# Seven quarter products per two batches: from lagging 64x64 quadrants to the whole TensorE array

## The chip, the cores and the metric

The kernel runs on one core of one Trainium2 chip. The metric is the device time of one execution in microseconds (us), as the median of several; lower is better. Executions of one kernel spread by almost 2%: the timed fast runs of before lie between 395.2 and 402.4 us over all submissions. A verdict needs 2% and a 95% interval from fast runs of the same rounds.

## The reference, cut to what matters

```python
def _attn_ref(q, k, v):                     # 8 batches, 12 heads, 448 tokens, head size 64
    scores = scale * np.matmul(q, k.transpose(0, 1, 3, 2)) - np.log(S)
    attn = 1.0 / (1.0 + np.exp(-scores))    # a sigmoid, no softmax
    return np.matmul(attn, v)

def _moe_ref(x, w_in, w_out):               # 3584 tokens, 768 -> 2048 -> 768
    h = x @ w_in
    g = h * (1.0 / (1.0 + np.exp(-h)))
    return g @ w_out
# x is the attention's output, heads side by side
```

Inputs and output are float32 in memory; the kernel computes in float16 with float32 sums.

## The kernel before

Names that the text uses. A **group** is four heads of one batch; there are 24, three to a batch. **S** is a score step of a group (seven of them; TensorE, then two sigmoids on ScalarE), **V** its values block (28 matmuls, then two evictions on VectorE). Two batches at a time, the first layer is computed with seven **quarter products** (a Strassen-like scheme) for each of eight output blocks: 56 products a pair, for three pairs, and **Q** is one of their matmuls. The second layer is done in 14 units of seven products, and **P** is one of their matmuls. (In the code, `S` is the number of tokens, 448.) The first two batches go through the first layer in the plain way at the start.

The program's order comes from a small scheduler that runs in Python while the kernel is built: it keeps an own clock per engine and issues what its clock says is ready. Its constants are assumptions about the chip, and they fix the order of every in-order queue. A product of 64x64 quadrants runs in two halves, since two row halves of the array may not write one PSUM bank together (the prediction cites where that is said): the upper rows go ahead, and the lower rows follow after a semaphore, mixed with the upper rows of the next product.

```python
    def lower_ready():
        if not fifo:
            return False
        q, c = fifo[0]
        return c > 0 or (q.left is not None and pl.t >= q.left + 700.0)

    def lane_step(p=None, c=0):

        low = fifo.popleft() if lower_ready() else None
        assert p is not None or low is not None
        N = max(([p.N] if p else []) + ([low[0].N] if low else []))

        def go():
            if p:
                p.last = p.mm(0, c)[-1]
            if low:
                if low[1] == 0:
                    wait = nc.tensor.nop()
                    left = low[0].last
                ins = low[0].mm(1, low[1])
                if low[1] == 0:
                    for a_, b_ in ((wait, left), (ins[0], wait)):
                        tc.add_manual_dep(
                            a_.ins, b_.ins.name,
                            mybir.DependencyInfo(mybir.DependencyClass.Sync, mybir.DependencyReason.DATA),
                            reason="the upper rows have left the bank",
                        )

        done = low is not None and low[1] == low[0].n - 1
        d = N / 2.4 + 2.5
        pl.pe(d, low[0].key if done else None, [], go)
        if p:
            fifo.append((p, c))
            pl.main += d * (0.2 if p.n == NQ else 1.0)
            if c == p.n - 1:
                p.left = pl.t

    def emit(p, bank_id, deps):

        p.bank = bank_id
        ff_wait(deps)
        while len(fifo) > (7.5 if p.n == NQ else 2.5 * p.n):
            drain_one()
        for c in range(p.n):
            lane_step(p, c)
            if (c + 1) % 2 == 0 or c == p.n - 1:
                between()


    def between():
        if todo:
            if some_tasks() or todo[0][0][:2] != "tp" or todo[0][1] < NHB * NQ:
                return
        if pl.main >= pace[0] and vis[0] < len(visits):
            if visit():
                pace[0] = max(pace[0] + pace[1], pl.main + 300.0)

```

A quarter product in this form is 3 x 2 x 2 matmuls of 64x64, and attention is visited between them:

```python
            def mm(h, c):
                return [
                    nc.tensor.matmul(
                        bank[64 * j_ : 64 * j_ + 64, :S], lhs[64 * h : 64 * h + 64, c, 64 * j_ : 64 * j_ + 64],
                        rhs[64 * h : 64 * h + 64, c, :],
                        start=(new and c == 0 and h == 0), stop=(h == 1 and c == NQ - 1), skip_group_check=True,
                    )
                    for j_ in range(2)
                ]
# ... the combinations on VectorE, the sigmoids on ScalarE, the products on GpSimd ...
            emit(p, ib, (hold(ib) if new else []) + self.deps_of(j, n))
```

K and Q of the groups 8 to 23 are turned by DMA: VectorE copies them into a staging tile (one for K, one for Q), a DMA transpose on SyncE's queue writes one of two buffers, and the next copy waits for the transpose before it:

```python
            x = (xk, xq)[z][ring(n)]
            dst = (kT, qT)[z][tring(n)]
            y = xp[z]
            lk = ("k", n) if w == "k" else ("q", n, None)
            m = before(n, lambda i: -1 if i in on_pe else 0)
            old = [("tr" + w, m)] if m is not None and m not in on_pe else []
            pl.op(
                "DVE", 530, ("re" + w, n), [lk] + old,
                lambda x=x, y=y: nc.vector.tensor_copy(
                    y.rearrange("p (c j d) -> p c j d", j=2, d=D), x.rearrange("p (j c d) -> p c j d", j=2, d=D)
                ), prio=-1,
            )
            pl.op(
                "SP", 1200, ("tr" + w, n),
                ([("trk", n)] if w == "q" and one else []) + [("re" + w, n)] + freed("S", n, NCH - 1, of=tring),
                lambda dst=dst, y=y: nc.sync.dma_start_transpose(dst, y), nbytes=1300,
            )
# ...
    visits = []
    for n in range(NHB * NQ, NALL):
        if n in on_pe and n >= 8:
            visits[-6:-6] = [("tk", n, 0), ("tq", n, 0)]
        for i in range(NCH):
            if i == 2 and n > NHB * NQ:
                visits.append(("V", n - 1, 0))
            visits.append(("S", n, i))
    visits.append(("V", NALL - 1, 0))
    vis = [0]
```

## Time and profile before

| before | |
|---|---|
| time, 4 runs | 401.38 us median (398.8 to 402.33) |
| profiled execution | 394.43 us, span 392.6, granted clock 0.998 |
| TensorE busy | 94% |
| VectorE, ScalarE, GpSimd busy | 67%, 63%, 36% |

The profiled execution is faster than all four timed ones. That matters later. In the profile, "PE" is TensorE, "PEld" its weight loads, "DVE" VectorE, "ACT" ScalarE, "POOL" GpSimd, "SP" SyncE with most output DMA; "issue" is idle time that no semaphore explains. The view of waits has one line per waiting engine and source line: what it waited for, us in total, times, longest. TensorE's waits of before, from 86 us to the end:

```profile
PE ps L905 <- issue: 5.5, 8, 1.1
PE ps L1028 <- issue: 1.7, 3, 1.1
PE ps L1028 <- DVE us L1042: 1.5, 1, 1.5
```

TensorE stands idle little, and mostly at Q for no reason that the profile names. What the waits can't show is a TensorE that is busy with only half of its rows.

### The profile page before, as it was taken

How to read it: one execution, taken by the hardware profiler on the slowest of the kernel's cores; microseconds unless marked ns; L12 is line 12 of the kernel's file. 1: busy time of each engine (PE TensorE's matmuls, PEld its weight loads, DVE VectorE, ACT ScalarE, POOL GpSimd, SP SyncE). 2: the span in 40 equal slices, each digit the busy share in tenths (PEclk: the TensorE clock that was granted, in tenths of full speed). 3: DMA queues.
4: the chain of work that ended last, by engine and by line, in shares of the span. 5: the costliest groups of instructions: out<-in, count | busy, mean ns of one | idle time of the engine just before them, and what ended most of it. 6: DMA issues, size and time to landing. Idle time of an engine off the chain costs nothing.

```text
span 392.6 us, 17870 instructions
## 1 busy us (share of the span) xinstructions
PE 368.0 (94%) x7724; PEld 292.7 (75%) x7724; DVE 264.2 (67%) x484; ACT 246.3 (63%) x562; POOL 142.2 (36%) x193
## 2 busy tenths in 40 slices
PE   6899999999998999998999998899999989899994
PEld 2677777889786676866887766788787676699993
DVE  2545888989454678877755687768466777775542
ACT  1886788578786967787857576689774456510100
POOL 8745302202222318775222057774000176620000
PEclk9999999999999999999999999999999999999999
DMA  8999995706999981345988907049952200013335
GB/s 103 200 209 203 209 208 87 99 2 103 183 185 207 165 139 27 48 64 72 179 139 153 215 8 92 3 55 156 156 112 56 52 3 3 2 39 88 85 83 122
DMA packets 63741, 42.30 MB, mean 108 GB/s; under 512 B 33712, under 2 KB 62896, under 8 KB 63664
## 3 DMA queue, kind: packets, MB, share of 16 engines
q0 software_dynamic: 25008, 22.81, 39.0%
q1 hardware_dynamic: 38656, 18.36, 24.9%
q8 instruction: 61, 1.00, 1.1%
q14 instruction: 16, 0.13, 0.1%
HBM read 45.61 MB, written 11.01 MB: 144 GB/s over the span
## 4 chain that ended last, share of the span: by engine, by line
PE 78%; DMA 7%; DVE 5%; ACT 5%; issue 4%; POOL 1%; SPq 0%; DVEq 0%; PEldq 0%; ACTq 0%; POOLq 0%
PE ps L1028 30%; PE ps L905 23%; PE ps L802 8%; PE ps L564 8%; PE ps L553 7%; DMA kT<-xp 3%; ACT at L601 2%; DMA xk<-in_k_dram 2%; ACT at L1182 1%; DMA qT<-xp 1%; DMA out_dram<-us 1%; PE ps L512 1%; DVE us L920 1%; ACT gt L706 1%; ACT gt L687 1%
## 5 line engine op out<-in xcount | busy, mean ns | idle before, releaser
L1028 PE MATMUL ps<-wo,gt 64*64 64x384 f16 x1792 | 140.9, 323 | 2.0 <-issue 1.5
L601 ACT ACTIVATE at<-ps 128x448 f16<-128x448 f32 x252 | 118.7, 589 | 29.2 <-PE ps L553 28.7
L1028 PEld LDWEIGHTS <-gt 64*64 64x64 f16 x2240 | 108.3, 107 | 18.4 <-issue 6.5
L711 POOL TENSOR_TENSOR gt<-us,gt 128x448 f16<-128x448 f32 (+4 forms) x96 | 77.2, 827 | 70.4 <-ACT gt L706 55.2
L905 PE MATMUL ps<-xt,wi 64*64 64x448 f16 x864 | 80.3, 350 | 1.6 <-issue 1.1
L1028 PE MATMUL ps<-so,gs 64*64 64x384 f16 x896 | 81.3, 323 | 0.2 <-issue 0.2
L553 PE MATMUL ps<-qT,kT 64*64 64x448 f16 (+2 forms) x728 | 71.5, 333 | 3.8 <-DMA qT<-xp 0.7
L920 DVE SCALAR_TENSOR_TENSOR us<-ps,us 128x448 f32<-128x448 f32 x96 | 58.1, 621 | 22.5 <-PE ps L905 17.0
L905 PEld LDWEIGHTS <-wi 64*64 64x64 f16 x1152 | 55.8, 106 | 20.2 <-issue 9.2
L905 PE MATMUL ps<-xs,ex 64*64 64x448 f16 x576 | 61.3, 351 | 1.6 <-issue 1.4
L1042 DVE TENSOR_TENSOR us<-ps,us 128x384 f32<-128x384 f32 x70 | 38.6, 555 | 34.8 <-PE ps L1028 29.5
L279 POOL DMA_DIRECT2D v<-in_v_dram x22 | 16.0, 727 | 118.1 <-PE ps L564 83.3
L706 ACT ACTIVATE gt<-us 128x448 f16<-128x448 f32 (+4 forms) x96 | 43.0, 484 | 17.5 <-DVE us L920 11.7
L1028 PEld LDWEIGHTS <-gs 64*64 64x64 f16 x896 | 49.7, 107 | 4.9 <-issue 1.1
L553 PEld LDWEIGHTS <-kT 64*64 64x64 f16 x728 | 34.3, 109 | 16.8 <-issue 12.4
L1028 PE MATMUL ps<-so,gt 64*64 64x384 f16 x448 | 43.7, 323 | 1.6 <-DVE us L1042 1.5
L802 PE MATMUL ps<-xt,wi 128*128 128x256 f16 (+1 forms) x384 | 40.9, 260 | 0.2 <-issue 0.2
L1182 ACT ACTIVATE at<-ps 128x384 f16<-128x384 f32 (+3 forms) x78 | 33.1, 532 | 10.3 <-PE ps L553 10.2
L905 PE MATMUL ps<-xs,wi 64*64 64x448 f16 x288 | 36.5, 351 | 2.4 <-issue 2.4
L905 PEld LDWEIGHTS <-ex 64*64 64x64 f16 x576 | 31.5, 106 | 8.3 <-issue 2.7
L564 PE MATMUL ps<-at,v 64*64 64x448 f16 (+2 forms) x688 | 36.8, 331 | 0.2 <-issue 0.2
L802 PEld LDWEIGHTS <-wi 128*128 128x128 f16 x384 | 33.0, 98 | 5.3 <-issue 1.7
(64 smaller groups left out, 424.4 us busy)
## 6 DMA issues: line engine op xcount, KB each, us to landing
out_dram<-us SPq DMA_DIRECT2D x112, 96.0 KB, 3.2
xk<-in_k_dram POOLq DMA_DIRECT2D x22, 224.0 KB, 5.3
v<-in_v_dram POOLq DMA_DIRECT2D x22, 224.0 KB, 4.3
xq<-in_q_dram POOLq DMA_DIRECT2D x20, 224.0 KB, 6.8
wo<-in_moe_w_out_dram POOLq DMA_DIRECT2D x4, 768.0 KB, 14.1
wi<-in_moe_w_in_dram POOLq DMA_DIRECT2D x8, 192.0 KB, 6.9
wi<-in_moe_w_in_dram POOLq DMA_DIRECT2D x4, 384.0 KB, 10.6
ex<-in_k_dram POOLq DMA_DIRECT2D x2, 224.0 KB, 6.7
```

The lines of the kernel that those rows point to most:

```text
L279: lambda: nc.gpsimd.dma_start(v16[vring(n)], src(v, b, g)),
L553: nc.tensor.matmul(pt[r][64 * h : 64 * h + 64, lo : lo + (c1 - c0) * D], kT[tring(n)][64 * r : 64 * r + 64, i, 64 * h : 64 * h + 64], qT[t ...
L564: nc.tensor.matmul(pt[h][64 * j : 64 * j + 64, :N], v16[vring(n)][64 * h : 64 * h + 64, j, c * D : (c + 1) * D], ats[slots[c]][64 * h : 64 ...
L601: lambda r=r: nc.scalar.activation(ats[sl][:, r], pt[r][:, :S], AF.Sigmoid, bias=NEG_LOG_S, scale=QKSCALE),
L706: lambda o=o, x_=x_: nc.scalar.activation(o, x_, AF.Sigmoid, scale=1.0 if in_sb else ISX), prio=0,
L711: lambda o=o, x_=x_: nc.gpsimd.tensor_tensor(o, x_, o, ALU.mult), prio=5,
L802: nc.tensor.matmul(bank[:, z * N : z * N + N], wi[:, cc, fc * P : (fc + 1) * P], x[:, cc, self.c0 : self.c1], start=(cc == 0 and z == 0), ...
L905: nc.tensor.matmul(bank[64 * j_ : 64 * j_ + 64, :S], lhs[64 * h : 64 * h + 64, c, 64 * j_ : 64 * j_ + 64], rhs[64 * h : 64 * h + 64, c, :] ...
L920: lambda: nc.vector.scalar_tensor_tensor(us[o], bank[:, :S], ISX, us[i_], ALU.mult, ALU.add), prio=-2,
L1028: nc.tensor.matmul(bank[64 * j : 64 * j + 64, :HE], lhs[64 * h : 64 * h + 64, c, 64 * j : 64 * j + 64], rhs[64 * h : 64 * h + 64, c, :], s ...
L1042: lambda: nc.vector.tensor_tensor(o, bank[:, :HE], u, add), prio=-2,
L1182: lambda r=r, src_=src_: nc.scalar.activation((at[:, base : base + m] if base < 8 else atx[:, base - 8 : base - 8 + m])[:, :, r, :N], src_ ...
```

## The change

The intent: a quarter product has 128 rows and 128 columns to offer, so it needn't be cut into quadrants. On the whole array there is no lag of rows and a quarter of the instructions. But the tiling mode changes whenever attention, which needs quadrants, comes between, so attention is kept out of those stages. Beside it, constants of the scheduler change.

```diff
-        return c > 0 or (q.left is not None and pl.t >= q.left + 700.0)
+        return c > 0 or (q.left is not None and pl.t >= q.left + 450.0)
 # ... (the same constant in two more places)
-            pl.main += d * (0.2 if p.n == NQ else 1.0)
+            pl.main += d * (0.0 if p.n == NQ else 1.0)
 # ...
-        if pl.main >= pace[0] and vis[0] < len(visits):
+        if pl.main >= pace[0] and vis[0] < len(visits) and (pl.mode == 2 or 0):
             if visit():
 # ...
-            def mm(h, c):
-                return [
+            def go():
+                for c in range(NQ):
                     nc.tensor.matmul(
-                        bank[64 * j_ : 64 * j_ + 64, :S], lhs[64 * h : 64 * h + 64, c, 64 * j_ : 64 * j_ + 64],
-                        rhs[64 * h : 64 * h + 64, c, :],
-                        start=(new and c == 0 and h == 0), stop=(h == 1 and c == NQ - 1), skip_group_check=True,
+                        bank[:, :S], lhs[:, c, :], rhs[:, c, :],
+                        start=(new and c == 0), stop=(c == NQ - 1), skip_group_check=True,
                     )
-                    for j_ in range(2)
-                ]
 # ...
-            emit(p, ib, (hold(ib) if new else []) + self.deps_of(j, n))
+            while fifo:
+                drain_one()
+            ff_wait((hold(ib) if new else []) + self.deps_of(j, n))
+            pl.pe(NQ * (S / 2.4 + 2.5), pk, [], go, mode=1)
+            between()
 # ...
-            R += [Q(1, z), Q(6, z), Q(7, y), Q(2, y), Q(5, z), Q(2, z), Q(7, z), Q(4, y), Q(3, y)]
-            tail = [Q(4, z), Q(3, z)]
+            R += [Q(1, z), Q(6, z), Q(7, y), Q(2, y), Q(5, z), Q(2, z), Q(7, z), Q(4, y), Q(3, y), Q(4, z), Q(3, z)]
+            tail = []
 # ...
-        return 0.2 * NQ * (S / 2.4 + 2.5) if w[0] == "s" else HFC * (HE / 2.4 + 2.5)
+        return 0.0 * NQ * (S / 2.4 + 2.5) if w[0] == "s" else HFC * (HE / 2.4 + 2.5)
 # ...
+        run_ = next((w for w in near if w[0] == "s" and g1[w[1]].started), None)
+        if run_ and near[0][0] == "s":
+            near = [w for w in near if w[0] == "s"]
 # ... (and 600 instead of 300 ns of slack for a quarter product while in whole-array mode)
```

More of the change, by code (lines that the diff above doesn't have):

```diff
@@ L453, in drain_one @@
         if c == 0:
-            pl.t = max(pl.t, q.left + 700.0)
+            pl.t = max(pl.t, q.left + 450.0)
             pl.flush()
@@ L901, in run @@
             }[n]
-            def mm(h, c):
-                return [
+            def go():
+                for c in range(NQ):
                     nc.tensor.matmul(
-                        bank[64 * j_ : 64 * j_ + 64, :S], lhs[64 * h : 64 * h + 64, c, 64 * j_ : 64 * j_ + 64],
-                        rhs[64 * h : 64 * h + 64, c, :],
-                        start=(new and c == 0 and h == 0), stop=(h == 1 and c == NQ - 1), skip_group_check=True,
-                    )
-                    for j_ in range(2)
-                ]
+                        bank[:, :S], lhs[:, c, :], rhs[:, c, :],
+                        start=(new and c == 0), stop=(c == NQ - 1), skip_group_check=True,
+                    )
             pk = ("Q", b, j, n)
-            p = Prod(pk, NQ, S, mm)
             done = None
@@ L1467 @@
         near = L[: 9]
+        run_ = next((w for w in near if w[0] == "s" and g1[w[1]].started), None)
+        if run_ and near[0][0] == "s":
+            near = [w for w in near if w[0] == "s"]
         z = next((y for y, w in enumerate(near) if due(w)), None)
         if z is None:
-            z = next((y for y, w in enumerate(near) if due(w, 300.0)), None)
+            z = next((y for y, w in enumerate(near) if due(w, 600.0 if pl.mode == 1 and w[0] == "s" else 300.0)), None)
         if z is None:
@@ L1478 @@
                 t = [pl.heap[0][0]] if pl.heap else []
-                t += [fifo[0][0].left + 700.0] if fifo and fifo[0][0].left is not None else []
+                t += [fifo[0][0].left + 450.0] if fifo and fifo[0][0].left is not None else []
                 pl.t = max(pl.t, min(t))
@@ L1482 @@
             z = 0
-        w = L.pop(z)
+        w = near[z]
+        L.remove(w)
         if w[0] == "s":
```

## The prediction

> **What bounds the kernel now.** I read the page first (engine totals, slices, costliest groups), then a table of busy time by stage, then the chain that ended last in order of time, then the queue that starts the DMA transposes. The words I use: P is a second-product matmul (line 1028), Q a quarter-product matmul of the first layer (line 905; 3 batch pairs of 56 products), S and V are the attention's scores and values (lines 553 and 564).
>
> The page's totals and two rows of its costliest groups (busy us, then mean ns):
> ```profile
> PE 368.0 (94%) x7724; PEld 292.7 (75%) x7724; DVE 264.2 (67%) x484; ACT 246.3 (63%) x562; POOL 142.2 (36%) x193
> ...
> L905 PE MATMUL ps<-xt,wi 64*64 64x448 f16 x864 | 80.3, 350 | 1.6 <-issue 1.1
> ...
> L802 PE MATMUL ps<-xt,wi 128*128 128x256 f16 (+1 forms) x384 | 40.9, 260 | 0.2 <-issue 0.2
> ```
> TensorE is the bound at 94% busy, but the two rows show why this cannot be read as 94% of its peak: a 64x64 matmul is in flight for 350 ns however many share the array. So I count array time: four quadrant matmuls, or one whole-array matmul, of N columns are one slot. Busy time by stage (boundaries are my choice, at the chain's changes between lines 1028 and 905):
> ```profile
> core 0: us, PE busy (x) PEld busy (x) DVE busy (x) ACT busy (x) POOL busy (x), PEclk, DMA share, GB/s
> 86.00:140.20 54.20, 52.00 (x1058) 41.32 (x1051) 33.52 (x61) 44.57 (x101) 12.20 (x17) 1.00 1.01 165
> 140.20:181.50 41.30, 38.05 (x776) 29.03 (x774) 32.31 (x65) 29.32 (x75) 28.69 (x37) 1.00 0.38 52
> 181.50:222.00 40.50, 39.28 (x850) 31.52 (x847) 26.96 (x47) 29.63 (x66) 9.04 (x13) 1.00 1.02 166
> 222.00:264.50 42.50, 40.20 (x815) 30.35 (x809) 32.14 (x58) 30.21 (x76) 28.14 (x42) 1.00 0.35 50
> 264.50:304.80 40.30, 39.44 (x861) 31.18 (x860) 26.12 (x44) 28.57 (x65) 6.19 (x8) 1.00 0.68 118
> 304.80:342.80 38.00, 34.86 (x706) 25.43 (x700) 27.98 (x48) 19.93 (x38) 21.32 (x21) 1.00 0.07 15
> 342.80:392.60 49.80, 44.83 (x1074) 42.95 (x1068) 25.70 (x44) 5.55 (x11) 3.07 (x4) 0.99 0.36 82
> ```
> P stages and Q stages alternate. The last row holds P alone: 1074 matmuls in 44.83 us, 167 ns a slot. The sixth holds almost only Q. Before its Q stage the chain (start, us, what) shows attention's data ending the first P stage, and in the last Q stage small gaps that no semaphore explains:
> ```profile
> 131.27 6.95 DMA kT<-xp
> ...
> 313.54 0.98 issue
> 314.53 6.17 PE ps L905 x123
> ...
> 328.07 6.21 PE ps L905 x123
> 334.28 0.58 issue
> 334.87 2.70 PE ps L905 x52
> ...
> 342.84 44.81 PE ps L1028 x1070
> ```
>
> **What the Trainium skill says.** (1) "TensorE: Matmul & The Clock Gate", Back-to-back issue gap: a warm matmul follows the last after N/2.4 + 2.5 ns. That is 189.2 ns for 448 columns and 162.5 for 384; the 167 ns above agree within 3%. (2) "TensorEngine Tiling (Array Packing)", Gotcha 1: different row tiles may not access one PSUM bank at the same time. This is why the kernel runs the lower rows of a product behind its upper rows, with a semaphore between; no trace can contradict it, as the kernel obeys. (3) The same page, Key Properties: changing the tiling mode drains TensorE. In the start-up, which already alternates modes, twelve 256-column whole-array matmuls hold the chain 1.42 us against 12 x 109.2 = 1.31, and the twenty 192-column quadrant matmuls after them 0.54 against 5 x 82.5 = 0.41. So a round trip costs about 0.24 us: it agrees, and is small. (4) The first page, LDWEIGHTS: the time is columns/1.2, so a 64-column load should take half of a 128-column one. The trace disagrees: 106 to 109 ns for 64x64 and 98 ns for 128x128. The measurement decides: a Q slot drops from four loads of 106 ns to one of 98, which 189 ns of matmul hide.
>
> **The change, part by part.**
> *Q on the whole array.* 3 x 56 x 12 = 2016 quadrant matmuls become 504, and as many loads with them; TensorE's program goes from 15450 rows to 12426. Array time does not change: 504 slots x 189.2 ns = 95.4 us both ways. What can go is only the loss around it. Counting slots in the built instruction order between the first and last Q of each pair, ideal against measured time:
> the P stage from 86.0 to the first Q at 135.2: 44.3 ideal, 49.2 measured;
> from there to the end, ideal 36.9 (first Q stage, with 10 score steps, one V block and 46 P) + 37.2 + 38.9 + 34.0 + 35.5 + 43.6 = 226.1 us; measured 387.7 - 135.2 = 252.5. So 26.4 us are lost there, and 4.9 us are stores after the last matmul.
> *Attention leaves the Q stages.* A visit now needs quadrant mode. In the built order the three Q stages hold 168 Q without a break but for two score steps each near the end of the first two; the P stages between hold 40 and 34 score steps (30 and 27 before) and 6 V blocks each (5 before). The P matmuls that were mixed into Q's ends (46, 92, 92) move into the P stages, the last becoming 1120.
>
> New stages:
> Q stage: 168 x 189.2 = 31.8 us of slots. VectorE has 6 operations per output block there; three of line 920 took 1.76 us in a row, so 6 x 0.59 = 3.5 us, against 21 slots = 4.0 us of TensorE. GpSimd has 3 products at 1.0 us, ScalarE 5 operations of about 0.5. So TensorE still bounds it, narrowly. With draining the lagging rows, two switches and the entry after the x sums I take 33.5 us (8 blocks x 4.05 + 1.1). Today's attention-free stage runs 4.7 us a block: from 318.6 to 337.3 us four blocks went by on VectorE's line 716.
> Second P stage: 672 P, 160 S, 168 V = 210 slots; 168 x 162.5 + 82 x 189.2 = 42.8 us. The first P stage, equally mixed, ran at 49.2/44.3 = 1.11 of ideal, today's second at 40.5/37.2 = 1.09. I take 47.
> Third P stage: 168 x 162.5 + 76 x 189.2 = 41.7, at 1.09: 45.5.
> Last P stage: 1120/4 x 167 = 46.8, then 4.9 of stores.
> Sum: 135.4 (unchanged up to the first Q) + 3 x 33.5 + 47 + 45.5 + 46.8 + 4.9 = 380.1 us of span. I add 1.5 us for the hand-over from the first Q stage to its P stage: unit 3 needs batch 2 whole, through VectorE, ScalarE, GpSimd and the sums, and the two products of Q that used to be held back to cover this are no longer held back. Predicted span 381.6, that is 11.0 less than 392.6, so 401.4 - 11.0 = **390.4 us**.
> *The shorter delay (700 to 450 ns) and the pace constants* change only the order of issue; real order is kept by the semaphores. I give them nothing.
>
> **Rivals.**
> *Attention's data become the bound of the P stages.* K and Q are transposed by DMA into two buffers, each transpose waiting for the scores two steps back and for its single staging buffer. Starts in the first P stage:
> ```profile
> 107.24 1.25 SPq L496 DMA_TRANSPOSE kT<-xp  x1
> ...
> 114.93 1.24 SPq L496 DMA_TRANSPOSE kT<-xp  x1
> ...
> 122.65 1.52 SPq L496 DMA_TRANSPOSE kT<-xp  x1
> ...
> 131.27 1.45 SPq L496 DMA_TRANSPOSE kT<-xp  x1
> ```
> 7.7 us seems the floor; the five periods from 88.0 to 131.27 average 8.65. The second P stage needs 40/7 = 5.7 heads-groups, 5.7 x 8.65 = 49 us against my 47; if each also waits on the fuller DMA (share 1.01 and 1.02 in the first two P stages, 0.35 to 0.38 in the Q stages, which could prefetch only two groups), two stages lose 2 to 4 us each: about 396. For it: the chain's 6.95 us. Against: groups are ready at the stage's start.
> *ScalarE becomes it.* A score step has two sigmoids; 22 in a row took 9.71 us, 0.44 each. 40 x 2 x 0.44 + 3 us of copies = 38 of 47 us: no, unless bunched.
> *VectorE bounds the Q stages.* At 0.62 us an operation, alone, a block takes 3.7 us; with transposed-input copies and x evictions in it 4.3 or more, so 35 to 36 us a stage: about 396.
> *Everything is hidden anyway:* the gaps return as other waits and only the issue gaps and mixed rows go; then 3 to 5 us, 397.
> *The better way:* P stages reach 1.05 of ideal: 47 becomes 45, 45.5 becomes 44, and with no hand-over loss: 385.
>
> **Range and chances.** The rivals put most of the outcomes between 385 and 396, and the three timed runs before spread over 3.5 us. Range 384 to 397. Faster by over 2% needs below 393.4, 3.0 us above my number: 0.66. Within 2%: 0.31. Slower by over 2% would need the P stages some 20 us longer, for which I see no cause: 0.03.
>
> **What would show it.** Right: Q matmuls as 128*128 x504 with 168 in 33 to 34.5 us per stage, VectorE near 90% busy there, the issue waits at Q (5.5 us before) nearly gone; P stages of 46 to 48 and 44 to 47 us; P alone at 167 ns a slot at the end; ScalarE busier in the P stages and nearly free of score sigmoids in the Q stages. Wrong: Q stages over 35 us with VectorE or GpSimd ending TensorE's waits; P stages over 49 us with transposes or sigmoids in the chain; or a first P stage that differs from 135 us, which I took as unchanged.

## The result, and the profile after

After takes **389.18 us** (median of 4 runs, 385.01 to 389.57) against 401.38 us. The ratio is **0.968, with a 95% interval of 0.960 to 0.976**: faster. A ratio is the mean time of one kernel's fast runs over the mean of the other's of the same rounds, so it isn't quite the ratio of the medians. All runs here were fast ones. In the profiled execution of after the granted clock was 0.984 on average, but 1.00 in every stage below: its slow stretches lie before 24 us and after the last matmul.

The page of after, engine totals and the first of the rows of Q (busy us, mean ns, idle before):

```profile
PE 366.1 (95%) x6212; PEld 260.9 (67%) x6212; DVE 263.1 (68%) x484; ACT 244.7 (63%) x562; POOL 141.6 (37%) x193
...
L905 PE MATMUL ps<-xt,wi 128*128 128x448 f16 x216 | 49.1, 353 | 1.1 <-DVE us L916 1.1
```

TensorE's busy share went *up* by a point while the kernel became faster, and a Q matmul still reads 353 ns (350 before): the share says nothing of how full the array is. The table by stage, as the prediction showed it for before. Stages are cut here at the first and last Q of each pair; the columns are those of the prediction's table.

```profile
85.50:133.95 48.45, 46.52 (x983) 37.39 (x975) 30.04 (x56) 40.23 (x92) 11.60 (x17) 1.00 1.06 163
133.95:168.15 34.20, 32.93 (x179) 16.57 (x177) 29.39 (x59) 22.27 (x60) 21.93 (x28) 1.00 0.26 45
168.15:220.61 52.46, 48.46 (x1001) 37.65 (x1000) 31.77 (x56) 39.66 (x90) 14.76 (x21) 1.00 0.97 153
220.61:253.26 32.65, 32.55 (x179) 16.59 (x176) 29.63 (x53) 22.27 (x57) 24.41 (x37) 1.00 0.28 43
253.26:301.84 48.58, 45.68 (x977) 37.30 (x977) 28.52 (x49) 36.18 (x84) 11.15 (x16) 1.00 0.70 119
301.84:334.49 32.65, 32.05 (x170) 16.35 (x168) 28.03 (x50) 19.30 (x38) 19.80 (x20) 1.00 0.06 13
334.49:382.40 47.91, 47.84 (x1121) 37.42 (x1120) 25.99 (x44) 6.42 (x13) 4.46 (x5) 1.00 0.32 74
```

Rows 2, 4 and 6 are the Q stages: 32.65 us twice for 168 slots of 189.2 ns = 31.8 us. Rows 3 and 5 are the P stages that now hold the attention: 52.5 and 48.6 us for 42.8 and 41.7 us of slots. In the view of waits, TensorE's waits in after, from 86 us on:

```profile
PE ps L1028 <- DVE us L1042: 3.6, 2, 2.0
PE ps L553 <- DMA qT<-xp: 2.6, 5, 0.9
PE ps L905 <- DVE us L916: 1.1, 1, 1.1
```

The "issue" waits at Q are gone; waits of the P stages for output buffers (line 1042) and for turned Q (qT) have grown. To compare kernels whose stages mix differently, I cut every trace at the first Q of each pair, where the same work lies between; the last column is the time from the third such mark to the last matmul.

| trace | first Q at | period 1 | period 2 | last period | its Q stages | P stages after them |
|---|---|---|---|---|---|---|
| before | 135.2 | 84.6 | 81.6 | 86.2 | mixed with attention and P | |
| before, second trace (e0) | 136.9 | 85.2 | 81.8 | 85.7 | mixed | |
| after | 133.9 | 86.7 | 81.2 | **80.5** | 34.3, 32.7, 32.7 | 52.4, 48.5, 47.8 |

The gain that the traces show stands in the last period, which has no attention in it: 5.2 to 5.7 us. The first two periods, with attention, gave nothing (+1.5 to +2.1 and -0.4 to -0.6). This was not what the prediction's sum says, and the experiments ask about it.

### The profile page after: what moved, and what is told of

Read it like the earlier page. It is cut to its first block, busy times and chain, and to the rows that moved or that the text cites. A ratio compares the mean times of both kernels' runs of the same rounds, so it can differ in the third digit from the quotient of the medians.

```text
span 387.2 us, 14682 instructions
## 1 busy us (share of the span) xinstructions
PE 366.1 (95%) x6212; PEld 260.9 (67%) x6212; DVE 263.1 (68%) x484; ACT 244.7 (63%) x562; POOL 141.6 (37%) x193
## 4 chain that ended last, share of the span: by engine, by line
PE 67%; DMA 17%; DVE 8%; POOL 2%; ACT 2%; issue 2%; SPq 1%; DVEq 0%; ACTq 0%; POOLq 0%; PEldq 0%
PE ps L1028 26%; PE ps L905 19%; PE ps L802 9%; DMA qT<-xp 7%; PE ps L564 6%; PE ps L553 6%; DMA kT<-xp 3%; DVE us L916 3%; DMA out_dram<-us 2%; DMA v<-in_v_dram 2%; DMA wi<-in_moe_w_in_dram 2%; DVE gt L716 1%; ACT gt L706 1%; DVE xp L489 1%; DVE us L942 1%
## 5 line engine op out<-in xcount | busy, mean ns | idle before, releaser
L1028 PE MATMUL ps<-wo,gt 64*64 64x384 f16 x1792 | 138.0, 323 | 0.3
L1028 PEld LDWEIGHTS <-gt 64*64 64x64 f16 x2240 | 103.8, 107 | 24.1 <-issue 8.8
L711 POOL TENSOR_TENSOR gt<-us,gt 128x448 f16<-128x448 f32 (+3 forms) x96 | 76.7, 828 | 63.1 <-ACT gt L706 44.6
L553 PE MATMUL ps<-qT,kT 64*64 64x448 f16 (+2 forms) x728 | 67.9, 334 | 3.9 <-DMA qT<-xp 2.6
L1042 DVE TENSOR_TENSOR us<-ps,us 128x384 f32<-128x384 f32 x70 | 38.6, 554 | 33.5 <-PE ps L1028 26.4
L706 ACT ACTIVATE gt<-us 128x448 f16<-128x448 f32 (+3 forms) x96 | 42.7, 480 | 29.1 <-DVE us L916 22.2
L1028 PEld LDWEIGHTS <-gs 64*64 64x64 f16 x896 | 51.3, 107 | 8.0 <-DVE gs L316 1.3
L905 PE MATMUL ps<-xt,wi 128*128 128x448 f16 x216 | 49.1, 353 | 1.1 <-DVE us L916 1.1
L905 PEld LDWEIGHTS <-wi 128*128 128x128 f16 x288 | 27.9, 98 | 27.9 <-issue 2.3
L802 PE MATMUL ps<-xt,wi 128*128 128x256 f16 (+1 forms) x384 | 40.8, 260 | 0.1
L612 DVE TENSOR_SCALAR xt<-ps 128x448 f16<-128x448 f32 x36 | 20.8, 620 | 28.5 <-PE ps L564 25.6
L1048 ACT ACTIVATE us<-ps 128x384 f32<-128x384 f32 x28 | 14.5, 517 | 35.8 <-PE ps L1028 35.3
L802 PEld LDWEIGHTS <-wi 128*128 128x128 f16 x384 | 33.0, 98 | 5.1 <-issue 1.4
L905 PE MATMUL ps<-xs,ex 128*128 128x448 f16 x144 | 34.6, 352 | 0.0
```

What stands on the lines that cost most here:

```text
L553: nc.tensor.matmul(pt[r][64 * h : 64 * h + 64, lo : lo + (c1 - c0) * D], kT[tring(n)][64 * r : 64 * r + 64, i, 64 * h : 64 * h + 64], qT[t ...
L612: lambda h=h: nc.vector.tensor_scalar_mul(xt[:, (2 * n + h) % XC, :], pt[h][:, :S], SX), prio=-2,
L706: lambda o=o, x_=x_: nc.scalar.activation(o, x_, AF.Sigmoid, scale=1.0 if in_sb else ISX), prio=0,
L711: lambda o=o, x_=x_: nc.gpsimd.tensor_tensor(o, x_, o, ALU.mult), prio=5,
L802: nc.tensor.matmul(bank[:, z * N : z * N + N], wi[:, cc, fc * P : (fc + 1) * P], x[:, cc, self.c0 : self.c1], start=(cc == 0 and z == 0), ...
L905: nc.tensor.matmul(bank[:, :S], lhs[:, c, :], rhs[:, c, :], start=(new and c == 0), stop=(c == NQ - 1), skip_group_check=True,)
```

## The experiments

Twelve runs were made. Two theories to begin with: **W**, the form of the quarter products (no row lag) brings the gain; **M**, moving the attention out of their stages brings it. For the P stages: **D/T**, late DMA data (stores, transposes) bound them; theory **P** (not the matmul of that name), TensorE's own order and mixing.

### e0: before, once more

No edit; it measures the spread and gives a second trace.

> The kernel before, unchanged. The profiled execution of before took 394.4 us, its four timed ones 398.8 to 402.3, so the traces differ by 5.4 us of span where the times differ by 12. Expected: ratio 1.00 within 0.01, and a second trace. If the profiled one was a lucky one, this trace has a span near 398 us and shows which stage holds the other 5 to 7 us: by the data theory the stages with attention (DMA transposes, loads and stores late), by the TensorE theory the quarter-product stages.

Measured: 399.59 us (396.95 to 401.44), ratio 1.001 (0.993 to 1.009). Its trace has a span of 395.2 us; its three timed executions had 397.7 to 399.6. So the profiled execution from which the prediction subtracted (392.6) was a lucky one: by 2.6 us against this trace and by 5 to 7 us against the timed executions. The second trace doesn't hold the missing time in one place: it reaches the first Q 1.7 us later, period 1 is 0.6 longer, the last one 0.5 shorter.

### a1: after, once more

No edit; it stands beside e6, e7 and e8 on the same chip.

> The changed kernel, unchanged, as the measure for the three beside it: 387 to 390 us, ratio to before 0.97. Its second P stage, between the first two quarter-product stages, took 52.5 us in the first trace where the prediction had 47, and the third 48.6 against 45.5; both should come back within 2 us.

Measured: three fast runs of 385.7, 386.6 and 391.0 us, ratio **0.976** (0.966 to 0.987). (The median of all four, 388.8 us, isn't used: it has a slow run in it.) That run, the profiled one, took 1277 us; nothing here explains it, and its trace is of no use, so what was expected of the stages stays unchecked by this run. The stages of e4, 51.8 and 47.1 us for the second and third P stage, repeat those of after instead.

### e2 and e3: one part of the change alone

e2 puts the Q matmuls back into lagging quadrants and keeps attention out:

```diff
-            while fifo:
-                drain_one()
-            ff_wait((hold(ib) if new else []) + self.deps_of(j, n))
-            pl.pe(NQ * (S / 2.4 + 2.5), pk, [], go, mode=1)
-            between()
+            emit(Prod(pk, NQ, S, mm), ib, (hold(ib) if new else []) + self.deps_of(j, n))   # mm as before
 # in emit:
-            if (c + 1) % 2 == 0 or c == p.n - 1:
+            if p.n != NQ and ((c + 1) % 2 == 0 or c == p.n - 1):
                 between()
```

> The changed kernel with the quarter products put back into lagging 64x64 quadrants, attention still kept out of them. Theory W (the form of the quarter products brings the gain): near before, 397 to 402 us. Theory M (moving attention out of the quarter-product stages brings it): near after, 388 to 392 us. In the trace by W: the last quarter-product stage at 36 to 38 us against 32.7 in after.

e3 keeps the whole array and lets attention back between the products:

```diff
-        if pl.main >= pace[0] and vis[0] < len(visits) and (pl.mode == 2 or 0):
+        if pl.main >= pace[0] and vis[0] < len(visits):
 # and Q again counts 0.2 of its time in the pace and in cost()
```

> The changed kernel with attention allowed back between the whole-array quarter products (10 and 6 score steps and one values block each in the first two such stages, against 2, 2 and none in after). W: 386 to 391 us, since the form is kept; the switches cost about 15 round trips of 0.24 us, 4 us, less than what the earlier start of attention gives to the stages after. M: 396 us or more.

Measured: e2 400.99 us, ratio **1.000** (0.992 to 1.009). e3 395.7 us (median of its three fast runs), ratio **0.991** (0.982 to 1.000). Neither theory stands alone: moving the attention brings nothing by itself, and the whole array with attention between its products brings 0.9%, which isn't clear of nothing. Only the two together give 0.968. (The profile of e3 fell in a slow execution, clock 0.967, so its long stages show nothing.)

The periods of the traces, cut as in the table above, say more. Those of e2 are 88.0, 83.8 and 84.2 us. Against before, keeping attention out of lagging quadrants made the first two 2 to 3.4 us longer and the last 1.5 to 2.0 us shorter. Against e2, the whole array made all three shorter, by 1.3, 2.6 and 3.7 us. And e3's last period, which has no attention, took 80.8 us even in its slow execution, near the 80.5 of after. So most of the last period's gain comes with the whole array alone. What needs both are the first two periods: with attention between whole-array products they were longer again (e12 below: 88.9 and 83.3 us against 86.7 and 81.2 in after).

What the lag costs is seen in the third Q stage, which has no attention in any kernel. The row of the table by stage for e2, then three lines of its chain there (start, us, what):

```profile
305.60:342.90 37.30, 35.93 (x704) 30.46 (x704) 31.00 (x54) 20.05 (x39) 20.22 (x20) 1.00 0.06 13
```

```profile
322.70 0.56 issue
323.26 6.17 PE ps L905 x122
329.44 0.15 issue
```

37.3 us against 32.65 in after, for 31.8 us of Q slots in both. Of the 5.5 us above the slots, about 1.3 us are 32 P matmuls that it shares lane steps with (704 matmuls less 672 Q, four to a slot of 162.5 ns), 1.4 us idle, and the rest, 2.8 us, is TensorE busy with part of the array empty. It isn't a lower rate of the stream: by the starts of the matmuls in the trace, 112 quadrants began between 323.5 and 328.8 us, 47.3 ns each, which is 189 ns for four and full. The loss lies where one half has no partner or both stop: about 0.7 us at the entry, 2 us at three breaks like the one at 322.70, and 1.6 us at the end, from 337.8 us on. After loses nothing in this stage before its last 2 us.

### e4 and e5: lag or number of instructions?

e4: no lag, but each whole-array matmul in two of 128 rows by 64 columns. e5 is e2 with each pair of columns as one matmul of 64 rows by 128 columns: lag, but half of the instructions. Both have 1008 Q matmuls.

```diff
 # e4, against after
                 for c in range(NQ):
-                    nc.tensor.matmul(bank[:, :S], lhs[:, c, :], rhs[:, c, :], ...)
+                    for j_ in range(2):
+                        nc.tensor.matmul(bank[64 * j_ : 64 * j_ + 64, :S], lhs[:, c, 64 * j_ : 64 * j_ + 64], rhs[:, c, :], ...)
 # e5, against e2
-                    nc.tensor.matmul(bank[64 * j_ : 64 * j_ + 64, :S], lhs[64 * h : 64 * h + 64, c, 64 * j_ : 64 * j_ + 64],
-                                     rhs[64 * h : 64 * h + 64, c, :], ...)      # for j_ in range(2)
+                    nc.tensor.matmul(bank[:, :S], lhs[64 * h : 64 * h + 64, c, :], rhs[64 * h : 64 * h + 64, c, :], ...)
```

> The changed kernel with each whole-array quarter-product matmul as two of 128 rows by 64 columns: no row lag, but twice the matmuls and loads (1008 against 504, 2016 in before). If the lag of the rows is what cost before its time: equal to after within 1%, 387 to 392 us, quarter-product stages of 32.5 to 34 us. If the number of instructions is what cost: a third of the way back, 392 to 395 us, stages of 34 to 36 us.

> The kernel of e2 (quarter products with lagging rows, attention kept out of them) with each pair of 64x64 column neighbours as one matmul of 64 rows by 128 columns: the row lag stays, the matmuls and loads halve to 1008. Together with e4 (1008 without lag, 0.970) it tells lag from count. If the lag is the cost: near e2 and before, ratio 0.99 to 1.01. If the count of instructions is the cost: near e4, 0.97 to 0.98. The borders, where P and quarter products share lane steps, now change the tiling mode at each step, which can add 1 to 3 us.

Measured: e4 387.68 us, ratio **0.970** (0.963 to 0.976), its Q stages 35.0, 32.8 and 32.8 us. e5 400.55 us, ratio **1.007** (0.999 to 1.015). e4 settles one half of the question: twice the matmuls without lag cost nothing. That e5 is as slow as before looks like the other half, but its stage row has more than lag in it, at 360 matmuls (336 Q):

```profile
306.40:344.60 38.20, 37.46 (x360) 21.59 (x360) 30.25 (x52) 20.69 (x39) 21.60 (x22) 1.00 0.05 12
```

TensorE is busy for 37.46 of 38.20 us, with hardly a wait. Yet its 336 half-array matmuls are 168 slots, 31.8 us, and the 24 P matmuls beside them one more. So some 4.7 us went by with TensorE busy and part of the array empty. The chain at the stage's entry (P is line 1025 here) shows what over half of it went into:

```profile
306.46 0.29 PE ps L905
306.75 0.28 PE ps L1025 x2
307.03 0.29 PE ps L905
307.32 0.28 PE ps L1025 x2
```

A Q of 64x128 and two P of 64x64 share a lane step here, and they run one after the other, 0.57 us a step, where e2's steps are all of 64x64 and run side by side. There are seven such steps at the two ends of this stage; at 0.57 less 0.18 us of slots each they cost 2.8 us (an estimate from these starts). By the same count, 19 steps in the whole kernel cost about 7 us. e5's expectation named this confounder (1 to 3 us), so 1.007 is not the price of lag alone, and e5 doesn't show that half of the instructions with lag bring nothing. What shows that the lag and not the count costs is e4, with e2's stream, which is full at four quadrants in 189 ns wherever both halves have work. No busy share shows the loss.

### e6 and e13: do stores or transposes bound the P stages?

The second P stage of after ends in a chain of DMA. Its chain there:

```profile
203.41 7.58 DMA out_dram<-us
...
212.22 4.58 DMA qT<-xp
...
217.50 1.32 PE ps L564 x28
```

A store takes 7.58 us (3.3 is the median), VectorE waits for the buffer that it frees, the staging copy of Q stands behind that in VectorE's queue, so the transpose starts at 212.2, and TensorE gets on at 216.9. e6 leaves out the stores of units 3 to 8 (wrong on purpose), e13 the transposes of groups 14 to 18 (wrong on purpose; the program order is otherwise the same).

```diff
 # e6, in store()
             def go():
+                if 3 <= self.pi <= 8:
+                    return
 # e13, in transpose_dma()
-                lambda dst=dst, y=y: nc.sync.dma_start_transpose(dst, y), nbytes=1300,
+                lambda dst=dst, y=y: None if 14 <= n <= 18 else nc.sync.dma_start_transpose(dst, y), nbytes=1300,
```

> The changed kernel with the output stores of units 3 to 8 left out (rows 768 to 2303 are wrong on purpose), program order otherwise the same. Theory D (in the second and third P stage the DMA engines are full, a store of 96 KB x 2 takes 7.6 us, VectorE waits for the buffer that it frees, and the copies that feed the next DMA transposes stand behind that wait): the second P stage falls from 52.5 to 47 to 49 us and the third by 1 to 2, in all 382 to 386 us. Theory P (the mixing of scores, values and P costs this on TensorE itself): 387 to 390, unchanged.

> The changed kernel without the DMA transposes of groups 14 to 18 (their scores use old K and Q: wrong on purpose), program order otherwise the same. It takes the transposes, their DMA time and every wait for them out of the second P stage. Theory T (late transposes bound that stage): 52.5 falls to 44 to 47 us, 381 to 384 in all. Theory P: 50 to 52, 386 to 389.

Measured: e6 386.34 us (0.971, 0.965 to 0.978; its output fails the check, as meant), second P stage 51.3 us, third 45.7. Its last period, in which every store is kept, is 2.3 us longer than after's (82.8), so that the whole time is no better than a1's 386.6 of the same rounds. e13 385.97 us (0.969, 0.961 to 0.977), second P stage 49.9, third 46.6; its output passed the check although its scores use old K and Q, so a passed check is no proof here that the transposes ran (its trace has one in the second P stage, after's eleven). Each takes 1 to 3 us out of a stage, not the 5.5 by which the second one missed the prediction. Theory T said 44 to 47; it falls as the whole cause, and so does the store. In each, the chain of the stage's end shows the other one. Of e6, then of e13:

```profile
208.88 6.10 DMA qT<-xp
```

```profile
202.21 6.75 DMA out_dram<-us
```

The loss has its places, though. For P alone, the second P stage of after in three parts (the first pair of numbers after the length is TensorE's busy time and count):

```profile
168.15:176.00 7.85, 5.32 (x74) 3.19 (x78) 1.00 0.60 90
176.00:204.00 28.00, 24.35 (x477) 18.30 (x473) 1.00 1.04 157
204.00:220.60 16.60, 8.94 (x137) 5.28 (x125) 1.00 1.04 176
```

With 24, 80 and 56 S matmuls and 28, 84 and 56 V matmuls from the same view (a matmul across a border counts in both parts), the slots come to 5.5 of 7.85 us, 27.1 of 28.0 and 10.9 of 16.6. The 28 us in the middle run at 97%. The loss is 2.4 us at the hand-over from the Q stage, and 5.7 us at the end. There TensorE stands idle for 2.0 us at P, for an output buffer behind the store, and for 0.5 us at S, for the turned Q; in the other 3 us it is busy with part of the array empty: 14 P alone from 215.1 to 216.4 us, 14 S alone from 218.8 us on.

### e7, e8 and e12: three attempts to shorten the P stages

e7 turns group 16 on TensorE (`on_pe` gets a 16). e8 tells the scheduler that a store lands later (`lat=4500` for units 0 to 8). e12 issues V of groups 11 and 17 ahead of S of 12 and 18, and puts S of 12 and 18 into the Q stages:

```diff
-            if i == 2 and n > NHB * NQ:
+            if i == (0 if n % (2 * NQ) == 0 else 2) and n > NHB * NQ:
                 visits.append(("V", n - 1, 0))
 # ... S of 12 and 18 not before 15 us after their transposes in the scheduler's time, and then also in whole-array mode
```

> The changed kernel with the K and Q of head group 16 (second P stage) transposed by TensorE instead of by DMA. It takes one of the four transposes with their 7.7 us chain out of that stage, for 56 small matmuls (about 1 us of TensorE) and two more VectorE copies. D: second P stage 2 to 4 us shorter, 384 to 387 us. P: 1 us longer, 389 to 391.

> The changed kernel with the scheduler told that a store of units 0 to 8 lands 4.5 us after its transfer instead of 0.92, so it orders VectorE's combinations that need a stored buffer later, and the copies for the transposes earlier; the work is the same. D: the wait of VectorE for stores in the second P stage (1.9 us with 7.6 us of DMA behind it) shrinks, stage 48 to 51 us, 384 to 388 us in all. P: unchanged, 387 to 390.

> The changed kernel with the values of groups 11 and 17 issued ahead of the scores of 12 and 18, and the scores of 12 and 18 issued inside the quarter-product stages (9 score steps in each of the first two instead of 2). In after, the second P stage ends with TensorE waiting for the transposes of group 18 although only group 17 is needed. Theory O (that order costs the end of the stage): the second P stage falls from 52.5 to 46 to 48 us, the quarter-product stages grow by 1 to 2 us each, 383 to 387 us in all. Theory P (slots and mixing bound it): stage shorter only by the moved 7 x 0.19 us, 387 to 390.

Measured: e7 395.93 us (0.997, 0.988 to 1.007), e8 391.6 (median of its three fast runs; 0.985, 0.976 to 0.994), e12 392.92 (0.989, 0.981 to 0.996). None is better than after, and all three expectations missed. The fast runs of e7 and e12 all lie above those of after and a1; those of e8 (389.2 to 393.1) overlap them, so that it lost isn't shown, and its profile is of a slow execution. e7's second P stage grew to 55.4 us: its trace has one wait of 4.3 us there for an output buffer behind a store of 6.70 us, where after has 2.0; why the store came so late I did not follow. e12 did what it was to do in the P stage, 48.1 us where after has 52.4, but its first two Q stages grew to 40.8 and 36.0 us, by 6.5 and 3.3 us for seven S more. This answers part of the question that e2 and e3 left. Its chain in the second Q stage (Q is line 909 here):

```profile
241.34 0.31 PE ps L553 x4
241.66 0.68 PE ps L909 x3
242.33 0.31 PE ps L553 x4
...
245.97 4.91 DMA kT<-xp
250.97 0.62 DVE xp L489
```

An S among whole-array products holds the chain for 0.31 us instead of 0.19, and six Q after one take 1.24 us instead of 1.13: 0.23 us for the two mode changes. The prediction's 0.24 was right, and with seven S more that is 1.6 us, to which their own slots add 1.3: 2.9 us. In the second Q stage this is nearly all of the 3.3 us. The chain does pass through a transpose of 4.91 us there, but VectorE did not wait for it, and TensorE waited for VectorE for 0.2 us only. In the first Q stage there is more. TensorE's waits there, then the chain:

```profile
PE ps L909 <- DVE us L920: 2.5, 1, 2.5
PE ps L909 <- DVE xs L316: 0.9, 1, 0.9
```

```profile
129.33 7.67 DMA kT<-xp
...
137.10 0.10 DVE xp L489
...
138.40 0.63 DVE us L920
139.03 0.04 issue
139.07 8.99 PE ps L909 x39
```

The staging copy (line 489) of a group waits in VectorE's in-order queue until the transpose before it has landed, VectorE idles for 2.5 us, and the combinations behind the copy, on which the next Q depend, wait as well. TensorE stands idle for 3.4 us, where the first Q stage of after has 1.3. So the copies can hold up a Q stage, and did so once here; whether they are why e3 gains so little, no fast trace shows.

### e9: the delay of 700 ns back

```diff
-        return c > 0 or (q.left is not None and pl.t >= q.left + 450.0)      # and in two more places
+        return c > 0 or (q.left is not None and pl.t >= q.left + 700.0)
```

> The changed kernel with the assumed delay before the lower rows put back from 450 to 700 ns, for the P stages that still lag. My prediction gave the constant nothing: same as after within 0.5%, ratio to before 0.970 to 0.976. Rival: it is worth about 2 us, since the first quarter product starts at 133.1 to 135.0 us in the traces of after and its variants and at 135.2 and 136.9 in the two of before; then 0.975 to 0.981, and a first quarter product at 135.5 or later.

Measured in 5 rounds: 397.57 us median, but half of its six runs were slow ones. The three fast ones are 391.3, 393.6 and 395.5 us; ratio **0.988** (0.980 to 0.997). Its interval lies above that of after's first measurement and overlaps that of the second, 0.966 to 0.987. The constant may be worth 1 to 2%; it isn't the nothing that I gave it, if this holds, and it isn't shown beyond doubt. The only trace is of a slow execution, in which a transpose of 10.97 us holds up the first Q stage; I draw no loss from it. Its last two periods, 79.9 and 80.2 us, are even so no longer than after's 81.2 and 80.5: if the constant costs time, it isn't there.

## Why the prediction was right

The time was 389.2 us for a predicted 390.4, inside the range, and the verdict was the likelier one. Step by step:

- **Q on the whole array.** Predicted 33.5 us a stage, measured 34.3, 32.7 and 32.7. VectorE was at 86 to 91% of these stages (29.39 of 34.20 us, 29.63 of 32.65, 28.03 of 32.65), near the 90% of the prediction, and TensorE still bounds them. Right. The reason given, the loss around the slots, was right too, and e4 with e2's trace names it: the row lag, not the instruction count. The issue waits at Q went from 5.5 us to none.
- **The last P stage and the stores.** Predicted 46.8 and 4.9, measured 47.9 and 4.8 (387.2 less 382.4).
- **The first P stage.** Predicted unchanged, first Q at 135.4; it came at 133.9 in after and at 132.5 to 135.0 in the fast traces of its variants. Right within the spread.
- **The second and third P stage: mis-sized.** The terms 47 and 45.5 of the sum measured 52.46 and 48.58, together 8.5 us too small (7.0 with the 1.5 us kept for the hand-over, which measured 2.4). The first rival, late data at 49 us or more, is nearer the measured stage, and a P stage over 49 us with transposes in its chain was one of the prediction's own signs of being wrong. But e6 and e13 show that neither the stores nor the transposes alone carry it. I had scaled by the ratio of the older stages, in which part of the attention lay elsewhere; with all of it inside, the second P stage ran at 97% of its slots in the middle and lost 5.7 us at its end, behind stores and transposes.
- **The base: mis-sized the other way.** I took 11.0 us off both the profiled span and the median time. The spans predicted and measured are 381.6 and 387.2 (383.0 to 387.2 over four runs), 5.6 us apart: 8.5 for the two P stages and 1.1 for the last one, less 1.0 for Q, 1.5 for the first stage and the 1.5 kept for the hand-over. Time and span then stand 8.8 us apart in the prediction (390.4 and 381.6) and 2.0 in the measurement, 6.8 us the other way, because the profiled execution of before was 5 to 7 us faster than its usual ones, as e0 shows. Two errors of 5.6 and 6.8 us cancelled; that the time came within 1.2 us is luck. The change itself took 12.2 us off between medians in the first measurement, and about 10 between the medians of fast runs in a1's.
- **Not seen: that the two halves of the change need each other.** The prediction priced attention's place by the mode changes (0.24 us a round trip, confirmed at 0.23). That attention's staging copies, in VectorE's in-order queue, can stop the Q behind them (3.4 us of waits in e12's first Q stage) was not in it, nor that moving attention out of lagging quadrants brings nothing (e2).
- **The constants.** "I give them nothing": e9 speaks against it, without settling it.

What stays open: which part of the second P stage's 5.7 us at its end is whose. Stores and transposes were taken out one at a time only. Where the 4 us lie between the difference of e0's trace and after's (395.2 and 387.2) and the 12.2 us of the medians, no trace shows. No version that I tried beats after; e4 equals it.

## What to carry to other kernels

Measure an array's use in slots, not in busy time: a stage in which row halves lag behind each other was 96% busy (35.93 of 37.30 us in e2) and, without its P, 10% longer than with the whole array. If one product fills the array, give it the array; and then keep work that needs another tiling mode out of that stage, and look for the in-order copies that feed it. Before a prediction subtracts anything from a traced execution, compare that execution with the timed ones.

## What the Trainium skill lacked or had wrong

- "TensorE: Matmul & The Clock Gate", LDWEIGHTS: columns/1.2 would give 53 ns for 64 columns. The runs show 107 ns for 64x64, 110 for 128x64, 94 for 64x128 and 98 for 128x128, so a narrower load wasn't a shorter one in these traces.
- "TensorEngine Tiling (Array Packing)", Key Properties, says that a mode change drains TensorE, and no size. Here a pair of changes cost 0.23 us (e12), and in e5 a 64x128 matmul and two of 64x64 in one lane step took 0.57 us, 0.22 more than their two slots one after the other.
- The same page, Gotcha 1, leaves the handling of row tiles that share a bank to software. It doesn't say that lagging them costs: 37.3 us, 1.3 of it P, against 32.7 for the same Q slots (e2), while column tiles sharing a bank ran at the rate of the whole array, 32.8 us (e4).
- "TensorE: Matmul & The Clock Gate", Back-to-back issue gap, calls N/2.4 + 2.5 ns the gap of an isolated matmul and says that for many columns it is too long for a stream of loads and matmuls, 131 ns being measured at 512. Here it held for such a stream: 155 whole-array matmuls of 448 columns in 29.43 us, 189.9 ns each against 189.2. This case has no whole-array stream of 512 columns.
